# A fused convolution and hard-swish layer: one 256-column matmul ahead of each first layer, and the halves of each pair issued in the other order

## The chip, the cores and the metric

The kernel runs on one core of a Trainium2 chip. The time is what the device takes for one launch, in microseconds (us); the lower the better. The engines are TensorE (PE in the profile; its weight loads are listed apart as PEld), VectorE (DVE), ScalarE (ACT), GpSimd (POOL) and SyncE (SP, which only issues DMAs here). They run side by side and wait for each other through semaphores.

## The reference

```python
# x: 8 x 4096 x 192, weight: 8 heads x 7 taps, w_in: 192 x 2048, w_out: 2048 x 192
w = softmax(weight, axis=-1)
x_pad = zeros(6 rows) ahead of each sequence
attn[b, s, h, g] = sum_k w[h, k] * x_pad[b, s + k, h, g]      # a causal 7-tap convolution
t = attn.reshape(32768, 192)
h = t @ w_in
g = h * clip(h + 3, 0, 6) / 6
out = g @ w_out                                               # 32768 x 192, float32
```

## The kernel before

The 32768 tokens are worked off in 32 blocks of 1024 (NB blocks, TB tokens). A block has three stages: the convolution on VectorE (line 921), the first layer on TensorE (line 508) with its hard-swish on ScalarE and VectorE (lines 302 and 306), and the second layer on TensorE (line 615). Block 0 is special: its weights are still being prepared, and its first layer runs in plain fp32 through `half_mm` (line 296). Blocks 1 to 31 go through `first_layer` and `second_layer` in one loop; the convolution of later blocks runs under the matmuls.

**The two halves of the array.** The 192 input features are laid out as 3 thirds (K3) of 64 partitions. Partitions 0 to 63 hold the first 512 tokens of the block, partitions 64 to 127 the other 512. A matmul of the first layer therefore contracts over 64 rows and uses half of the TensorE array. In the code k is the half: k = 0 is rows 0 to 63, called the upper half of the array in this document, and k = 1 is rows 64 to 127, called the lower half. The two matmuls of a pair (k = 0 and k = 1) go to different halves and to different banks of PSUM, and they can run at the same time.

**The first layer.** `first_layer` walks over 16 chunks n, of 128 hidden features for either half. The first eight use `y_own` (the block's tokens as they lie), the other eight `y_other`, a copy in which the two halves of the partitions are exchanged by DMA. To get fp32 accuracy out of the single-pass data type float32r, activations and weights are split in three parts (HIGH, LOW and MIX), and each chunk needs three products. Each product is one call of `mms`: 3 thirds x 2 halves = 6 matmuls of 64 rows x 512 columns, so three pairs. A chunk has nine pairs and a first layer has 144. Below, pairs are counted from 0 in the order in which they are issued.

`begin(n)` takes a slot of PSUM (two banks), issues HIGH and LOW, and then multiplies both banks by 4097 (line 520, on ScalarE; for the last chunk lines 523 and 524, where VectorE takes one bank). `end(n)` issues MIX onto the multiplied sums and then runs the gate. So MIX of a chunk waits for the multiply, which waits for the last matmul of LOW. The order of the work is written out by hand: begin(0), begin(1), and then end(n) and begin(n + 2) in turn. In pairs: 0 to 5 are HIGH and LOW of chunk 0, 6 to 11 those of chunk 1, 12 to 14 are MIX of chunk 0, 15 to 20 HIGH and LOW of chunk 2, 21 to 23 MIX of chunk 1, and so on. Between begin(0) and end(0) there are the six pairs of begin(1); later there are nine pairs between a chunk's LOW and its MIX.

**The second layer.** It works on column strips of 32 output features (`tile_position=(0, j * 32)`), four streams side by side, in plain fp32.

**Weights.** Each matmul has a weight load of its own, issued ahead of it; the profile shows it as LDWEIGHTS on PEld.

Of the kernel before, what the change touches and what calls it, by code (L numbers as in the profile page):

```python
# [25 lines left out]
def kernel(  # L26
# [8 lines left out]
    nc = tc.nc  # L35
# [7 lines left out]
    N = 512  # L43
    G = 2
    TB = G * N
    D2 = P // 2
# [41 lines left out]
    for base, dma in ((0, nc.scalar), (D2, nc.sync)):  # L88
        dma.dma_start(  # L89
            out=w_sb[base : base + D2],  # L90
# [127 lines left out]
    for n in range(AHEAD):  # L218
# [8 lines left out]
        out=e_sb[:], in0=w_sb[:], in1=mx[:].to_broadcast([P, KC]), op=ALU.subtract  # L227
# [4 lines left out]
    half = cst.tile([P, 1], F32, name="half")  # L232
# [45 lines left out]
    psum = ps.tile([P, 2 * 4, N], F32, name="psum")  # L278
# [22 lines left out]
    def relu(r6, h):  # L301
        nc.scalar.activation(r6, h, ACT.Relu, bias=half[:], scale=1.0 / 6.0)  # L302

    def gate(g_, h):

        nc.vector.scalar_tensor_tensor(  # L306
            out=g_, in0=g_, scalar=1.0, in1=h, op0=ALU.min, op1=ALU.mult
        )
# [93 lines left out]
    def g_sums(engine, which, slots, width):  # L402

        forms = {
            3: (S3, A11, A21, ALU.subtract),
            2: (S2, S1, A11, ALU.subtract), 4: (S3, A12, S2, ALU.subtract),
        }
        for n in which:
            o, a, b, op = forms[n]
            for p in slots[::width]:  # L410
                r = slice(p, p + width)
                engine.tensor_tensor(out=o[:, r], in0=a[:, r], in1=b[:, r], op=op)  # L412
# [42 lines left out]
    def add(out, x, y, op=ALU.add):  # L455
        nc.vector.tensor_tensor(out=out, in0=x, in1=y, op=op)  # L456
# [13 lines left out]
    def r32(ap):  # L470
        return ap.bitcast(F32R)
# [16 lines left out]
    y_own, y_other, pools, s1 = [], [None], [], []  # L488
# [7 lines left out]
    def first_layer(i, jobs):  # L496

        slots = {}

        def both(n):  # L500
            return psum[:, 2 * slots[n] : 2 * slots[n] + 2]

        def mms(n, part, start=False, stop=False):
            group, c = divmod(n, NP)
            for s in range(K3):
                for k in range(2):
                    r = slice(k * D2, (k + 1) * D2)
                    nc.tensor.matmul(  # L508
                        out=psum[:, 2 * slots[n] + k], lhsT=r32(w_in_parts[part][r, c, s]),
                        rhs=r32(y_other[0][r, part, s] if group else y_own[part][r, s]),  # L510
                        start=start and s == 0, stop=stop and s == K3 - 1,
                        skip_group_check=True,
                    )

        def begin(n):
            slots[n] = free_slots.pop(0)
            mms(n, HIGH, start=True)
            mms(n, LOW)
            if n + 1 < count:
                nc.scalar.mul(both(n), both(n), 4097.0)  # L520
            else:
                lower, upper = (psum[:, 2 * slots[n] + k] for k in range(2))
                nc.scalar.mul(lower, lower, 4097.0)
                nc.vector.tensor_scalar(
                    out=upper, in0=upper, scalar1=4097.0, scalar2=None, op0=ALU.mult
                )

        def end(n):
            group, c = divmod(n, NP)
            mms(n, MIX, stop=True)  # L530
            to = g4[:, c, 1:3] if group else g4[:, c, 0::3]
            relu(to, both(n))
            gate(to, both(n))
            free_slots.append(slots[n])

        count = 2 * NP
        begin(0)
        begin(1)
        for job in jobs.get(-1, ()):
            job()  # L540
        for n in range(count):
            if n == count - 3:
                begin(n + 2)
            end(n)
            if n < count - 3:
                begin(n + 2)
            for job in jobs.get(n, ()):
                job()
            if n == 1:
                s1.append(ot.tile([P, NP, N], F32, name="s1", tag="shared")[:])  # L550
            if n < NP and n % 2:
                small_sums(s1[-1], A11, (1, 2, 3, 4), nc.gpsimd, every[n - 1 : n + 1])
            if n > NP and n % 2:
                pair = slice(n - NP - 1, n - NP + 1)
                g_sums(nc.gpsimd if n + 1 < count else nc.vector, (3,), range(NP)[pair], 2)
                if n + 3 < count:
                    nc.gpsimd.dma_start(out=S1[:, pair], in_=A22[:, pair], accum_op=ALU.add)
        for pair in (slice(NP - 2, NP), slice(NP - 4, NP - 2)):
            add(S1[:, pair], A21[:, pair], A22[:, pair])
# [7 lines left out]
    def small_sums(to, x, which, engine=nc.gpsimd, r=every):  # L567

        r = slice(r[0], r[-1] + 1)
        x11, x12, x21, x22 = four_parts(x[:, r])  # L570
        s1, s2, s3, s4 = four_parts(to[:, r])
        forms = {
            1: (s1, x21, x22, ALU.add), 2: (s2, s1, x11, ALU.subtract),
            3: (s3, x11, x21, ALU.subtract), 4: (s4, x12, s2, ALU.subtract),
        }
        for n in which:
            o, p, q, op = forms[n]
            engine.tensor_tensor(out=o, in0=p, in1=q, op=op)  # L578
# [222 lines left out]
    with tc.manual_schedule():  # L801
# [4 lines left out]
            out=c_sb[:], in0=e_sb[:], in1=sm[:].to_broadcast([P, KC]), op=ALU.mult  # L806
# [15 lines left out]
        for _ in range(3):  # L822

            nc.tensor.matmul(
                out=psum[:, b], lhsT=zeros[:, 0:P], rhs=zeros[:], start=True, stop=True
# [57 lines left out]
        slots = [0, 1, 3, 4, 6, 7, 9, 10, 12, 13]  # L883
        n = 3
# [30 lines left out]
        w_in_parts = [late.tile([P, NP, K3, P], F32, name=f"w_in{n}") for n in range(3)]  # L915
# [103 lines left out]
```

## Time and profile before

| | |
|---|---|
| time, median of 3 runs | 2226.65 us (2226.6 to 2228.04) |
| span of the profiled execution, first to last instruction | 2224.9 us |
| mean granted TensorE clock | 0.999 |
| first layer, line 508: matmuls | 8928, 386 and 388 ns each on average |
| second layer, line 615: matmuls of 128x512 on g and w_out | 6712, 552 ns each |
| multiply by 4097, line 520 | 465 on ScalarE, 1008 ns each |
| one block (start of line 508 at 510.08 us to the next at 578.46) | 68.4 us, of which 32.9 in the first layer |

The profile gives matmuls by start and modelled end. The ends of matmuls overlap, since they are pipelined; the pace of the stream is read from start to start. A row of the timeline merges instructions of one kind: start, length from the first start to the last end, engine, line, operation, operands, shape, and how many. In brackets stands the idle time of that engine ahead of the row, and what ended it. In the list of waits each row gives who waited for whom, the total in us, how often, and the longest.

### The profile page before, as it was taken

What the parts mean: (1) busy time and instruction counts of PE and PEld (TensorE: products, weight loads), DVE (VectorE), ACT (ScalarE), POOL (GpSimd) and SP (SyncE); (2) the same over time, 40 slices, a digit from 0 to 9 for tenths busy, and PEclk for the clock granted to TensorE, in tenths of its full rate; (3) what the DMA queues carried; (4) which work ended last, traced back from release to release, by engine and by line L of the source; (5) the groups of instructions that cost most, each with busy time, mean ns of one, the idle gap of its engine ahead of it and who ended that gap; (6) DMA issues with size and microseconds to landing.
All of it is one profiled execution on the core that took longest, in us unless ns stands there. A gap on an engine that the chain in (4) does not pass through costs nothing.

```text
span 2224.9 us, 50339 instructions
## 1 busy us (share of the span) xinstructions
PE 2218.0 (100%) x21496; PEld 1532.7 (69%) x21496; DVE 1894.3 (85%) x1673; ACT 1379.2 (62%) x1678; POOL 823.8 (37%) x690
## 2 busy tenths in 40 slices
PE   9999999999999999999999999999999999999999
PEld 5467776677766777766777667776677776677766
DVE  8888888888888888888888888888888888888876
ACT  7457665576655676555766557665567655576654
POOL 2344432344422444223443234442244422344323
PEclk9999999999999999999999999999999999999999
DMA  6244224443244342344422444324434234442232
GB/s 157 57 98 85 49 58 91 85 83 62 53 82 91 77 80 47 71 91 84 85 48 58 91 87 81 67 49 82 91 79 81 47 67 91 84 84 52 55 77 34
DMA packets 253584, 166.57 MB, mean 75 GB/s; under 512 B 208017, under 2 KB 213137, under 8 KB 253361
## 3 DMA queue, kind: packets, MB, share of 16 engines
q1 hardware_dynamic: 234872, 129.46, 28.4%
q0 software_dynamic: 17248, 33.64, 8.7%
q8 instruction: 168, 2.75, 0.5%
q14 instruction: 56, 0.45, 0.1%
q10 hardware_dynamic: 1240, 0.27, 0.1%
HBM read 31.72 MB, written 25.17 MB: 26 GB/s over the span
## 4 chain that ended last, share of the span: by engine, by line
PE 99%; DVE 0%; DMA 0%; ACTq 0%; issue 0%; DVEq 0%; ACT 0%
PE psum L615 49%; PE psum L508 46%; PE psum L296 2%; PE psum L341 2%; DMA x<-in_x_dram 0%; DVE y L255 0%; DVE top L175 0%; ACTq L89 0%; PE psum L816 0%; DVE results L456 0%; DVE scale L171 0%; DVE y L251 0%; DVE scale L192 0%; DVEq L1014 0%; DVE results L462 0%
## 5 line engine op out<-in xcount | busy, mean ns | idle before, releaser
L615 PE MATMUL psum<-g,w_out 128*32 128x512 f32 (+1 forms) x6712 | 967.5, 552 | 0.0
L306 DVE SCALAR_TENSOR_TENSOR g<-g,psum 128x1024 f32<-128x1024 f32 (+1 forms) x528 | 618.3, 1186 | 198.8 <-ACT g L302 194.5
L578 POOL TENSOR_TENSOR s<-g 128x256 f32<-128x256 f32 x248 | 273.6, 1103 | 1241.1 <-DVE g L306 1200.5
L302 ACT ACTIVATE g<-psum,half 128x1024 f32<-128x1024 f32 (+1 forms) x528 | 564.8, 1087 | 6.0 <-PE psum L508 5.2
L615 PEld LDWEIGHTS psum<-g,w_out 128*32 128x32 f32 x6712 | 371.8, 110 | 246.0 <-issue 126.7
L508 PE MATMUL psum<-y,w_in 64*128 64x512 f32 x4464 | 521.4, 388 | 0.0
L508 PE MATMUL psum<-y_other,w_in 64*128 64x512 f32 x4464 | 516.0, 386 | 0.0
L520 ACT ACTIVATE psum<-psum 128x1024 f32<-128x1024 f32 x465 | 469.0, 1008 | 50.7 <-PE psum L508 48.4
L508 PEld LDWEIGHTS psum<-y,w_in 64*128 64x128 f32 x4464 | 413.5, 184 | 115.7 <-issue 26.0
L508 PEld LDWEIGHTS psum<-y_other,w_in 64*128 64x128 f32 x4464 | 418.1, 184 | 87.8
L615 PE MATMUL psum<-s,w_out 128*32 128x512 f32 (+1 forms) x3272 | 465.5, 570 | 0.0
L921 DVE SCALAR_TENSOR_TENSOR y<-x,c_sb,y 128x1536 f32<-128x1536 f32 x186 | 335.2, 1802 | 2.6 <-ACT y L919 1.3
L412 POOL TENSOR_TENSOR s<-g 128x1024 f32<-128x1024 f32 x93 | 285.9, 3074 | 26.2 <-DVE g L306 26.2
L615 PE MATMUL psum<-g,w_s 128*32 128x256 f32 x1240 | 282.8, 379 | 0.0
L615 PEld LDWEIGHTS psum<-s,w_out 128*32 128x32 f32 x3272 | 154.3, 110 | 81.9 <-issue 49.4
L615 PEld LDWEIGHTS psum<-g,w_s 128*32 128x32 f32 x1240 | 136.4, 110 | 67.7
L412 DVE TENSOR_TENSOR s<-g 128x2048 f32<-128x2048 f32 (+1 forms) x93 | 181.3, 1977 | 1.1
L615 PE MATMUL psum<-s,w_s 128*32 128x256 f32 x744 | 170.7, 379 | 0.0
L578 DVE TENSOR_TENSOR g<-g 128x1024 f32<-128x1024 f32 x124 | 151.7, 1224 | 5.3
L412 DVE TENSOR_TENSOR g<-g 128x2048 f32<-128x2048 f32 x62 | 139.1, 2284 | 0.0
L612 ACT COPY psum<-psum 32x512 f32<-32x512 f32 x93 | 51.3, 551 | 135.4 <-PE psum L615 135.4
L456 DVE TENSOR_TENSOR results<-psum,results 32x256 f32<-32x256 f32 (+3 forms) x128 | 69.3, 541 | 50.9 <-issue 45.5
(91 smaller groups left out, 1299.5 us busy)
## 6 DMA issues: line engine op xcount, KB each, us to landing
y_other<-y SPq DMA_DIRECT2D x186, 384.0 KB, 5.1
g<-g POOLq DMA_DIRECT2D x62, 512.0 KB, 5.0
out_dram<-results SPq DMA_DIRECT2D x378, 64.0 KB, 2.0
x<-in_x_dram SPq DMA_DIRECT2D x53, 388.5 KB, 7.7
stage<-in_moe_w_in_dram SPq DMA_DIRECT2D x16, 192.0 KB, 4.5
stage<-in_moe_w_out_dram SPq DMA_DIRECT2D x8, 384.0 KB, 6.8
x<-in_x_dram SPq DMA_DIRECT2D x7, 384.0 KB, 8.4
x<-in_x_dram POOLq DMA_DIRECT2D x2, 388.5 KB, 5.4
```

Of the source, the lines that this page charges most:

```text
L296: nc.tensor.matmul(out=psum[:, b], lhsT=w[r], rhs=src, start=start, stop=stop, skip_group_check=onto,)
L302: nc.scalar.activation(r6, h, ACT.Relu, bias=half[:], scale=1.0 / 6.0)
L306: nc.vector.scalar_tensor_tensor(out=g_, in0=g_, scalar=1.0, in1=h, op0=ALU.min, op1=ALU.mult)
L341: lambda p=p: nc.tensor.matmul(out=bank[j * QS : (j + 1) * QS, tokens], lhsT=w_out[:, p, w, cols], rhs=x[:, p, tokens], start=(first and p ...
L412: engine.tensor_tensor(out=o[:, r], in0=a[:, r], in1=b[:, r], op=op)
L456: nc.vector.tensor_tensor(out=out, in0=x, in1=y, op=op)
L508: nc.tensor.matmul(out=psum[:, 2 * slots[n] + k], lhsT=r32(w_in_parts[part][r, c, s]), rhs=r32(y_other[0][r, part, s] if group else y_own[ ...
L520: nc.scalar.mul(both(n), both(n), 4097.0)
L578: engine.tensor_tensor(out=o, in0=p, in1=q, op=op)
L612: streams[3].append((t - 0.5, lambda: fn(*args, **kw)))
L615: nc.tensor.matmul(out=out, lhsT=w, rhs=x, start=start, stop=True, tile_position=(0, j * QS), skip_group_check=True,)
L921: jobs.append(lambda k=k: nc.vector.scalar_tensor_tensor(out=y[:], in0=x[:, :, k : k + N], scalar=c_sb[:, k : k + 1], in1=y[:], op0=ALU.mu ...
```

## The change

Ahead of the first pair of each first layer, one more matmul is issued. It goes to the upper half (rows 0 to 63), with the weights and activations of the first real matmul there, but with 256 columns instead of 512. It writes the left half of the bank that the first real matmul of the upper half then overwrites (`start=True`), so its result is not used. And in each pair the lower half (k = 1) is now issued ahead of the upper (k = 0). The changed kernel's lines from here on stand 8 lines further down.

```diff
         def mms(n, part, start=False, stop=False):
             group, c = divmod(n, NP)
+            if n == 0 and start:
+
+                r, half = slice(0, D2), slice(0, N // 2)
+                nc.tensor.matmul(
+                    out=psum[:, 2 * slots[n], half], lhsT=r32(w_in_parts[part][r, c, 0]),
+                    rhs=r32(y_own[part][r, 0, half]), start=True, stop=False,
+                    skip_group_check=True,
+                )
             for s in range(K3):
-                for k in range(2):
+                for k in (1, 0):
                     r = slice(k * D2, (k + 1) * D2)
                     nc.tensor.matmul(
                         out=psum[:, 2 * slots[n] + k], lhsT=r32(w_in_parts[part][r, c, s]),
```

## The prediction

> **What bounds the kernel now.** I read the page's busy times and its chain first, then the groups of line 508, then TensorE's timeline around one first layer, then the list of waits.
>
> ```profile
> PE 2218.0 (100%) x21496; PEld 1532.7 (69%) x21496; DVE 1894.3 (85%) x1673; ACT 1379.2 (62%) x1678; POOL 823.8 (37%) x690
> PEclk9999999999999999999999999999999999999999
> PE 99%; DVE 0%; DMA 0%; ACTq 0%; issue 0%; DVEq 0%; ACT 0%
> L508 PE MATMUL psum<-y,w_in 64*128 64x512 f32 x4464 | 521.4, 388 | 0.0
> L508 PE MATMUL psum<-y_other,w_in 64*128 64x512 f32 x4464 | 516.0, 386 | 0.0
> ```
>
> TensorE is busy over the whole span at an undisturbed clock, and 99% of the chain that ended last is its work, 46% of the span at line 508. So whatever lengthens or shortens TensorE's stream in a first layer is paid at the end. There are 8928 matmuls at line 508, 288 (144 pairs) in each of 31 first layers.
>
> The next answer is TensorE's timeline over the first layer at 510 us, in three cuts: its start with the other engines, its start for weight loads alone, and its second half.
>
> ```profile
> 510.08 2.60 PEld L508 LDWEIGHTS psum<-y,w_in 64*128 64x128 f32 x24 [0.84 <-issue]
> 510.09 3.48 PE L508 MATMUL psum<-y,w_in 64*128 64x512 f32 x28
> ...
> 511.79 1.01 ACT L520 ACTIVATE psum<-psum 128x1024 f32<-128x1024 f32 x1 [1.02 <-PE psum L508]
> ...
> 512.85 1.22 PEld L508 LDWEIGHTS psum<-y,w_in 64*128 64x128 f32 x12 [0.16 <-ACT psum L520]
> ...
> 527.94 15.12 PE L508 MATMUL psum<-y_other,w_in 64*128 64x512 f32 x132
> ```
>
> The last line holds 66 pairs: (15.12 - 0.386) us over 65 steps is 226.7 ns a pair. The first pair's two matmuls are recorded 3 ns apart (510.086 and 510.089 in the single records), and so is every later pair: the halves run in step. In the opening it goes a little slower: pair 5 (counted from 0) starts at 511.348, 1.262 us after pair 0, of which 0.110 is the exposed first weight load, so 230.4 ns a pair.
>
> The middle lines are what matters most here. The multiply of line 520 waits for pair 5, the last of chunk 0's low part (ends 511.743), runs from 511.785 to 512.793, and the weight load of pair 12 (chunk 0's mix part) waits for it until 512.845, with the matmul at 512.948. Without the wait pair 12 would have come at 512.945. That chain is just as long as the six pairs it has to hide behind. It recurs in every block, as the list of waits says:
>
> ```profile
> PEld psum L508 <- ACT psum L520: 5.0, 31, 0.2
> ```
>
> The single records add one thing: the lower half's weight load of pair 12 carries no wait of its own, had a free place since 512.721, and yet is issued at 512.848, 3 ns behind the waiting one. Here nothing passes the load that waits for a semaphore.
>
> **The change, part by part.** (1) The added matmul, 31 times: 256 columns in the upper half (rows 0 to 63). Its weight load takes the place of pair 0's exposed one (110 ns, there before too), and the upper half's real first load hides under it. Its length is not in the trace. Half of a 512-column pair step is 113 ns; at the other end, 256-column matmuls of line 615, which run in plain fp32, follow each other every 216 ns on one column strip. I take 113, the row of the same data type, and keep 216 for the range. The lower half starts pair 0 at the same time as the added matmul, so that from there the upper half trails the lower by about 113 ns.
>
> (2) The offset of the halves. What a pair costs when the halves are half a step apart is not shown for this data type. The nearest rows are the fp32 pairs of line 296 in block 0, same 64-row shape, which ran in step at first and out of step later:
>
> ```profile
> 19.04 1.88 PE L296 MATMUL psum<-y,w_in 64*128 64x512 f32 x8
> ...
> 42.40 0.59 PE L296 MATMUL psum<-y_swapped,w_in 64*128 64x512 f32 x1
> 42.51 0.59 PE L296 MATMUL psum<-y,w_in 64*128 64x512 f32 x1
> 42.83 4.99 PE L296 MATMUL psum<-y_swapped,w_in 64*128 64x512 f32 x22
> ```
>
> In step: (1.88 - 0.596) / 3 = 0.428 us. Apart by 0.11: (4.99 - 0.589 - 0.107) / 10 = 0.429. The offset is neither a gain nor a loss there. Those rows also bound the gain: a step of 429 ns is two passes of 512 columns, 214.6 ns a pass, so at best the 226.7 falls to 214.6. A loss has no row; I bound it by the worst single pair steps of the opening, 236 ns. I take no change.
>
> The Trainium skill's page "TensorE: Matmul & The Clock Gate" (section "Back-to-back issue gap") states N/2.4 + 2.5 ns, 215.8 ns at 512 columns, below this case's 226.7; by it the pair step could fall by 11 ns if being in step is what costs them. The same page (section "What overlaps and what doesn't") says that matmuls start and end strictly in program order, which speaks against the change, since a stall of one half then holds the other.
>
> (3) What becomes of the offset at pair 12. The upper half is now the later one, so pair 5 is finished 113 ns later; line 520 starts 113 ns later, and pair 12's first load, now the lower half's, is released at 512.958 instead of 512.845. The lower half's matmul goes at 513.061, the upper half's load is issued 3 ns behind the released one, and its matmul goes at 513.064. Left to itself the lower half would have started at 512.945 and the upper at 513.058. So the lower half loses the whole 113 ns, the upper half some 6, and **both leave pair 12 in step again**. The remaining 132 pairs of the layer run as before, with the roles of the halves exchanged. If the offset did shorten the first pairs, say to 214.6, pair 5 would come 5 x (230.4 - 214.6) = 79 ns earlier and the delay at pair 12 would be 34 ns, but the halves would be in step just the same: the lower's own time for pair 12 is then earlier still. The offset survives only if a pair takes so long (about 231 ns over the first twelve) that line 520 is no longer late.
>
> (4) The order within pairs. Lower first is the mirror image; I cost it at nothing, on the ground that either half's 144 matmuls at line 508 have the same form. If that ground is gone, rival B prices it.
>
> (5) What hangs on it. Queued behind the waiting load on TensorE is everything; DVE's gates and ACT's next multiplies come later by the same 113 ns. The next such chain has room: pair 21's mix load was issued at 514.795 and its multiply ended at 514.219, 576 ns ahead. The other engines and the DMA queues keep their instructions and their order; nothing is moved past a queue. The first loads that read y_other now wait for the lower half's transfer first, but no wait of line 508 for a DMA stands in the list of waits, so I cost that at nothing; a late transfer would show there.
>
> **Sum.** 113 ns a block x 31 = 3.5 us; from below 34 x 31 = 1.1, from above 216 x 31 = 6.7. TensorE has no idle time in which a block could make it up. The profiled execution's span is 2224.9, 1.75 below the median of the three runs (2226.65), and the same addition holds for both: span 2228.4, time **2230.1 us**, +0.16%. I count as no change what lies within 0.2% (4.45 us, 2222.2 to 2231.1), about what a measurement of this kernel can tell from none.
>
> **The rivals.**
>
> A. The offset lives through the layer and removes what a pair in step has above the best row. Per block 144 x (226.7 - 214.6) = 1742 ns less, 113 more: 1.63 us, x 31 = 50 us, **2176 us**. For it: r32 pairs take 12 ns more per 512 columns than fp32 pairs, and after each exposed load there are some seven irregular pairs (224 to 236 ns) before 226.7 sets in, so small differences in phase do count. Against it: the wait of pair 12 in every block, and the fp32 rows, which gain nothing when apart. It decides if pair 12 leaves more than a few ns between the halves.
>
> B. Slower: with the lower half leading, the irregular state of the opening doesn't settle. Pairs 1 to 7 average 231.5 ns ((511.811 - 510.422) / 6). Over the 132 pairs after the wait that is 132 x 4.8 = 634 ns a block, x 31 = 19.6, with the 3.5 above **2250 us**. For it: the settled 226.7 is a state that the halves fall into after a few pairs, so it hangs on how they start. Against it: they fell into it twice a block in all 31 blocks. It makes the kernel measurably slower from 0.24 ns a pair (0.95 us over 31 x 132 pairs).
>
> C. The added matmul costs more than the half step, 144 ns or more: at 216 it is **2233 us**. A smaller form of the forecast's own mechanism, on the other side of 0.2%.
>
> D. The offset neither dies nor matters: the added matmul's 113 ns once a block, 2230 again; told apart only by the trace.
>
> **How the numbers follow.** Forecast (with D) 0.66, of which 0.07 end above 2231.1 by a dearer start: its own range 2227.5 to 2232. Rival A and smaller gains of its kind 0.13. B and other losses per pair 0.13. C 0.08. Faster 0.13; slower 0.07 + 0.13 + 0.08 = 0.28; same 0.59. The range leaves out A (0.13) and the worst of B (0.06) and so ends at B's 2250; below, it goes to 2225, the forecast's lower bound (2227.7) less the spread of the runs.
>
> **What would show it.** In the timeline of a first layer of the changed kernel (its lines stand 8 further down): 31 matmuls more, with 256 columns; in pairs 0 to 11 the halves some 113 ns apart; the wait of the weight loads for line 520 grown from 0.16 to about 0.27 us in all 31 blocks, in which the upper half's last matmul delays it; after it matmuls in twos 3 ns apart again and 226.7 ns a pair; blocks of 68.49 instead of 68.37 us. The prediction is wrong if the halves are still apart after pair 12, if the step there isn't 226.7, or if the added matmul holds the upper half for much longer than 113 ns.

## The result, and the profile after

The changed kernel takes 2230.22 us in the median against 2226.68 us of the kernel before in the same set of runs: a ratio of 1.0016, with a 95% interval of 1.0009 to 1.0022. That is 3.5 us more, and it lies inside the 0.2% that were taken as no change. The spans of the profiled executions are 2228.3 against 2224.9 us. The times of one and the same kernel scatter by up to 2.0 us between runs and sets of runs (before: 2226.4 to 2228.4), and its spans with them (2224.8 to 2226.6), so where a microsecond matters the period of a block inside the profiled execution is used below: it repeats to the nanosecond in most blocks.

The page of the changed kernel; lines 508, 516 and 528 are now the added matmul, the pairs and the multiply by 4097:

```profile
span 2228.3 us, 50401 instructions
PE 2221.0 (100%) x21527; PEld 1560.8 (70%) x21527; DVE 1894.3 (85%) x1673; ACT 1379.2 (62%) x1678; POOL 823.6 (37%) x690
PEclk9999999999999999999999999999999999999999
PE 99%; DMA 0%; DVE 0%; SPq 0%; ACT 0%; issue 0%; DVEq 0%; ACTq 0%
L516 PE MATMUL psum<-y,w_in 64*128 64x512 f32 x4464 | 524.9, 388 | 0.0
L516 PE MATMUL psum<-y_other,w_in 64*128 64x512 f32 x4464 | 516.1, 386 | 0.0
```

TensorE has 31 matmuls more and is busy 3.0 us longer. The weight loads are busy 28 us longer; 14 of these lie in pairs 0 to 11, where loads of halves that are apart no longer cover each other, and the rest is spread over the whole run and not accounted for. DVE, ACT and POOL are as before. The matmuls on y_other, the second half of each first layer, cost what they did (516.1 us, before 516.0). What changed lies in the first half. The timeline of the same first layer, TensorE and ScalarE:

```profile
510.67 0.18 PEld L508 LDWEIGHTS psum<-y,w_in 64*128 64x128 f32 x1 [0.84 <-issue]
510.67 0.38 PE L508 MATMUL psum<-y,w_in 64*128 64x256 f32 x1
...
512.48 1.01 ACT L528 ACTIVATE psum<-psum 128x1024 f32<-128x1024 f32 x1 [1.13 <-PE psum L516]
...
513.54 0.77 PEld L516 LDWEIGHTS psum<-y,w_in 64*128 64x128 f32 x8
...
528.63 15.12 PE L516 MATMUL psum<-y_other,w_in 64*128 64x512 f32 x132
```

The last row is the same as before to the hundredth: 132 matmuls in 15.12 us, 226.7 ns a pair. The multiply starts 1.813 us after the first matmul of the layer, before 1.699: 114 ns later. The single records show what the rows merge. Each number is the recorded start of a matmul, in ns from the first one of the layer; a matmul that finds its weights not loaded yet is recorded about 110 ns ahead of its work (pair 0, and the lower half's pair 12, whose record lasts 497 ns where 386 is the rule):

```
                pair 0       1       2   ...      10      11        12          13          14         16
before, upper:       0     336     567          2405    2632      2862        3096        3320       3787
before, lower:       3     340     570          2409    2635      2865        3100        3324       3790
after, added:        0
after, lower:        3     338     568          2419    2646      2874+110    3212        3448       3908
after, upper:      223     458     691          2536    2763      2988        3224        3453       3916
```

From pair 0 to pair 11 the halves are 110 to 126 ns apart, with the lower one ahead. Pair 12's weight loads, at 2873 and 2876, come only after the multiply. The lower half's matmul begins work at 2984, the upper one's at 2988: 4 ns apart. From there the halves run together, 3 to 12 ns apart. In 29 of the 31 first layers pair 12 stands at these times to 1 ns; in the other two the halves leave it 2 ns apart, but draw apart over the pairs behind it to 43 ns, and keep these to the last pair. One block takes 68.487 us, before 68.373: 114 ns more, 31 times, 3.5 us.

### The profile page after: what moved, and what is told of

Same layout as the page of the kernel before. It is cut to its first block, busy times and chain, and to the rows that moved or that the text cites. A ratio compares the mean times of both kernels' runs of the same rounds, so it can differ in the third digit from the quotient of the medians.

```text
span 2228.3 us, 50401 instructions
## 1 busy us (share of the span) xinstructions
PE 2221.0 (100%) x21527; PEld 1560.8 (70%) x21527; DVE 1894.3 (85%) x1673; ACT 1379.2 (62%) x1678; POOL 823.6 (37%) x690
## 4 chain that ended last, share of the span: by engine, by line
PE 99%; DMA 0%; DVE 0%; SPq 0%; ACT 0%; issue 0%; DVEq 0%; ACTq 0%
PE psum L623 49%; PE psum L516 46%; PE psum L296 2%; PE psum L341 2%; PE psum L508 0%; DMA x<-in_x_dram 0%; SPq L100 0%; SPq L133 0%; DVE top L175 0%; PE psum L824 0%; DVE y L255 0%; DVE results L456 0%; SPq L89 0%; ACT y L838 0%; ACT scale L186 0%
## 5 line engine op out<-in xcount | busy, mean ns | idle before, releaser
L516 PE MATMUL psum<-y_other,w_in 64*128 64x512 f32 x4464 | 516.1, 386 | 0.0
L516 PEld LDWEIGHTS psum<-y,w_in 64*128 64x128 f32 x4464 | 435.4, 184 | 71.2 <-ACT psum L528 0.3
L516 PEld LDWEIGHTS psum<-y_other,w_in 64*128 64x128 f32 x4464 | 423.8, 184 | 82.1
```

Source lines behind the costliest of these rows:

```text
L516: nc.tensor.matmul(out=psum[:, 2 * slots[n] + k], lhsT=r32(w_in_parts[part][r, c, s]), rhs=r32(y_other[0][r, part, s] if group else y_own[ ...
```

## The experiments

**The order alone.** The kernel before with the lower half first.

```diff
-                for k in range(2):
+                for k in (1, 0):
```

> The lower half first in each pair, without the added matmul. Theory: mirror image, 226.7 ns a pair in step, 2226.7 us. Rival (the order in the pair has a price or gain of its own that is hidden in the 3.5 us): anything over 1 us away from that, with the added matmul then worth the rest.

Span 2224.9 us, as before; a ratio of 0.9999 (0.999 to 1.0009). A block takes 68.373 us, the same to the nanosecond. The halves go into their settled state as they did with the upper half first. So the order in the pair is worth nothing, and rival B has fallen.

**The added matmul alone**, with the upper half first as before.

```diff
-                for k in (1, 0):
+                for k in range(2):
```

> The added matmul with the upper half still first in each pair. The lower half's first matmul then stands in program order behind the upper half's first real one, so the halves never get apart. Theory (the price is the added columns alone): 113 ns a block as in the changed kernel, 2230.2 us, and no longer wait at pair 12 than before (0.16 us). Rival (the price comes from the offset and the longer wait at pair 12): 2226.7 to 2228 us.

Span 2228.3 us, the same 3.4 us above; median 2230.1, a ratio of 1.0009 (1.0 to 1.0019) in a set in which before stood at 2228.05, so 2.0 us by the medians. A block takes 68.480 us, 107 ns more than before, and the wait of the weight loads at pair 12 is in the list nearly as before (5.2 us, 31 times, against 5.0). The price doesn't need the new order. But the expectation was wrong in one thing: the halves did get apart, so this run doesn't show a price without an offset. The records show a second matmul 7 ns after the added one and the next at 224 ns, then one every 115 ns or so; in pair 12 the halves are some 20 ns apart and from pair 13 on 4.

**Which half is which.** The trace doesn't name the half, so the two kernels were run once more with the lower half's matmuls of chunk 0 cut to 508 columns.

```diff
+                    cols = slice(0, N - 4) if n == 0 and k else slice(0, N)
                     nc.tensor.matmul(
-                        out=psum[:, 2 * slots[n] + k], lhsT=...
+                        out=psum[:, 2 * slots[n] + k, cols], lhsT=...
```

> The run with the upper half first and the added matmul, with the lower half's matmuls of chunk 0 cut to 508 columns, so that the trace tells the halves apart; the last 4 columns of the lower half's sums of chunk 0 are left out. In that run the halves got 110 ns apart, which the expectation denied. Reading 1 (the lower half's first matmul starts ahead of the upper half's, which stands before it in program order but finds its half taken): the 64x508 matmul stands 3 to 7 ns after the added one, the upper half's 64x512 some 220 ns after it. Reading 2 (program order holds): the 64x512 first, at 220 ns, and the 64x508 not before it. The time: about 2230 us, as without the marks.

The timeline of the run with the upper half first, cut to the first 0.2 us of a layer:

```profile
510.82 0.38 PE L508 MATMUL psum<-y,w_in 64*128 64x256 f32 x1
510.82 0.49 PE L517 MATMUL psum<-y,w_in 64*128 64x508 f32 x1
```

The 64x508 matmul stands 7 ns after the added one; its record holds the 110 ns of an exposed weight load, so it works from about 117. The upper half's first 64x512 comes at 223 ns, though the program has it ahead of the 64x508. Reading 1 holds: a matmul whose half is free starts ahead of an earlier one whose half is taken, here by 216 ns between the records and by about 106 ns in work. What waits for the results still goes by the program: the upper half's last matmul of pair 5 ends at 1776 ns, the lower half's, which is last in the program and alone carries the signal, at 1630, and the multiply starts at 1821. It didn't run ahead of the slower half. The time was 2231.0 us.

> The changed kernel with the same mark (the lower half's matmuls of chunk 0 with 508 columns; the same 4 columns left out). It shows which half waits at pair 12. Theory: up to pair 11 the upper half's matmuls come some 110 ns after the lower's; at pair 12 the 64x508 matmul is held back by about 113 ns against the 226.7 ns step, the 64x512 by less than 10 ns, and they go 3 to 4 ns apart. Rival (the upper half is held as well): both held back by 100 ns or more and the offset kept. The time: about 2230 us.

At pair 11 the lower half's matmul starts at 2633 and the upper's at 2763. At pair 12 the 64x508 matmul is recorded at 2874 with 110 ns of waiting for its weights, so it works from 2984; it would have been due at 2633 + 227 = 2860 and is held by 124 ns. The 64x512 starts at 2989, 226 ns after its predecessor: not held at all. The two are then 5 ns apart. This is the collapse that the prediction worked out. The time was 2230.16 us.

This run shows one thing more. Over the irregular pairs behind the wait its lower half gets a little ahead once more: 30 ns from pair 16 on. No other weight load of the layer is held up, and in all 31 first layers the halves are still 30 ns apart in the last pair. The second half of the same layer:

```profile
528.54 15.15 PE L517 MATMUL psum<-y_other,w_in 64*128 64x512 f32 x132
```

The row is 0.03 us longer than the 15.12 of the halves in step, which is the offset itself: (15.15 - 0.386 - 0.030) / 65 is 226.7 ns a pair.

**The same columns without an offset.** Two added matmuls, one in each half (against the kernel before; the order in the pairs is that of the changed kernel).

```diff
+            if n == 0 and start:
...
+                for k in (1, 0):
+                    r, half = slice(k * D2, (k + 1) * D2), slice(0, N // 2)
+                    nc.tensor.matmul(
+                        out=psum[:, 2 * slots[n] + k, half], lhsT=...
```

> The changed kernel with an added 256-column matmul ahead of the layer in either half, so that the halves start in step. Theory (the price is the time of the added columns, whether they put the halves apart or not): 31 x 113 ns = 3.5 us above before, as the changed kernel, 2230 to 2231 us where before is 2226.7 to 2228, and the halves 3 ns apart from the first pair on. Rival (the offset and its loss at pair 12 carry part of the price): less than 2 us above before; or, if a second added matmul costs an issue of its own, over 4.5 us above.

Span 2228.4 us, 3.5 above; a ratio of 1.0021 (1.0012 to 1.003). A block takes 68.480 us, 107 ns more. The halves start 3 ns apart and stay so, and the weight loads' wait in pair 12 is that of the kernel before, as the list of waits of this run says:

```profile
PEld psum L509 <- issue: 26.0, 31, 0.8
PEld psum L517 <- ACT psum L529: 5.1, 31, 0.2
```

The added pair takes one step of 113 ns (pair 0 stands 223 ns behind it, of which 110 are the exposed weight load), and the two added matmuls are 3 ns apart, so the second one costs no issue of its own here. So the price is the time of 256 columns, paid at once here and paid through pair 12 in the changed kernel. The times alone would not say so: the medians of this set are 4.5 us apart (2231.24 against 2226.70), just on the rival's line. The profiled execution is the shortest of eleven; the others have spans of 2229.2 to 2229.9 us, and no trace shows where their extra microsecond lies.

**Twice the columns.** The added matmul with 512 instead of 256.

```diff
-                r, half = slice(0, D2), slice(0, N // 2)
+                r, half = slice(0, D2), slice(0, N)
```

> The changed kernel with 512 instead of 256 columns in the added matmul. Theory (the price is the added columns): twice 113 ns a block, 31 x 0.227 = 7.0 us above before, 2233.7 us. Rival (the price is one more instruction and its weight load, whatever its size): 2230.2 us.

Span 2232.2 us, 7.3 above; a ratio of 1.0028 (1.0017 to 1.0039), 6.1 us between the medians of the set. A block takes 68.613 us, 240 ns more against 114 with half the columns. The price goes with the columns, not with the instruction.

**The offset kept alive.** begin(2) is moved ahead of end(0), so that the multiply of chunk 0 has twelve pairs to hide behind. The control is the same move in the kernel before.

```diff
         begin(0)
         begin(1)
+        begin(2)
...
-            if n < count - 3:
+            if 0 < n < count - 3:
                 begin(n + 2)
```

> The changed kernel with begin(2) moved ahead of end(0), so that twelve pairs instead of six lie between the low part of chunk 0 and its mix part, and the wait that put the halves back in step has room. First theory (the offset dies only at that wait, and while it lives a pair takes the 230.8 ns that pairs 1 to 11 of the changed kernel show): halves about 110 ns apart all through the layer, 230.8 ns a pair, so 144 x 4.1 + 113 = 0.70 us a block above before, about 2248 us. Rival 1 (apart, the pairs settle at 226.7 ns as they do in step): 2230 us. Rival 2 (being in step is what costs 12 ns a pair, and the opening pairs were not yet settled): 214.6 ns a pair, about 2176 us. If another wait puts the halves in step, 2229 to 2230 us with the place to be seen in the trace.

> The kernel before with begin(2) moved ahead of end(0): the same reordering without the offset, as the control. Theory: no wait of weight loads for the multiply, and no irregular pairs 12 to 19, which cost some 33 ns a block above 226.7 ns each: 31 x 0.033 = 1.0 us less than before, 2225.7 us. Rival (irregular pairs come from the layer's schedule, not from the wait): 2226.7 us. If the third slot isn't free in time, a new wait at pair 12 and more than 2227 us.

Both are slower than before, for a reason of their own: 2242.77 us, a ratio of 1.0065 (1.005 to 1.008), and 2238.15 us, 1.0045 (1.003 to 1.006). The move takes the wait of pair 12 away and makes a longer one at pair 33, where a slot of PSUM isn't free yet. The list of waits of the run with the offset, and of the control:

```profile
PEld psum L516 <- DVE g L306: 16.0, 31, 0.5
```

```profile
PEld psum L508 <- DVE g L306: 16.2, 31, 0.5
```

So the expected gain of the control was not measured, nor was this offset kept through a whole layer: at pair 33 the matmuls of both halves are held, and leave it 4 ns apart. But up to there it did live, which is what the run was for. The timeline of that stretch, cut to pairs 10 to 29, in one row:

```profile
515.16 4.69 PE L516 MATMUL psum<-y,w_in 64*128 64x512 f32 x39
```

One matmul follows the other every (4.69 - 0.386) / 38 = 113.3 ns, the halves in turn, so a pair takes 226.5 ns apart (226.6 by the single records, which aren't rounded) as it takes 226.7 in step. The opening is slower in this run too (224 to 236 ns a pair up to some 2.4 us into the layer). My first theory, that pairs apart take 230.8 ns, took the opening for the offset; rival 1 of the expectation was right. At the end the offset costs its price as elsewhere: span 2240.0 against 2236.4 in the control, 3.6 us (4.6 by the medians).

**One half alone.** Both matmuls of a pair in the upper half.

```diff
-                    r = slice(k * D2, (k + 1) * D2)
+                    r = slice(0, D2)
```

> The kernel before with both matmuls of each pair in the upper half of the array (rows 0 to 63), one after the other; the lower half does nothing, so the sums of the second 512 tokens are left out and the first ones written twice. It measures the pace of a single half. Theory (a 512-column float32r matmul takes 226.7 ns in its half whether or not the other half runs): 288 x 226.7 = 65.3 us for a first layer, about 3240 us in all. Rival (the 12 ns above the fp32 rows are the price of two halves in step): 214.6 to 216 ns each, 61.8 to 62.2 us for a first layer, 3130 to 3145 us.

It took 3237.75 us, as the theory said. The timeline of the second half of a first layer, cut at 760 us:

```profile
741.29 18.97 PE L508 MATMUL psum<-y_other,w_in 64*128 64x512 f32 x83
```

(18.97 - 0.386) / 82 = 226.6 ns for one matmul with nothing beside it. There is nothing for an offset to win: the 12 ns above half of an fp32 step belong to the stream of float32r matmuls in one half, each with its weight load, and not to two halves in step. The irregular opening is there too with one half alone (224 to 236 ns a step up to 2.4 us, then 226.7).

## Why the prediction was right

**The bound.** Right: TensorE's stream gives back nothing, and 114 ns a block appear as 3.4 us in the span and 3.5 in the median.

**The added matmul (1).** I took 113 ns, half a pair step of float32r. In the changed kernel a block grew by 114. Where the added columns are paid directly (both halves), their step is 113 ns too; the block there grew by 107, because pairs 0 to 11 behind them take 6 ns less than before (2516 against 2522 ns from the start of work). The bound of 216, from the fp32 rows, was far off. (In the table ahead of the prediction the 6712 matmuls of line 615 are two forms: 5440 of 512 columns, 593 ns each, and 1272 of 256 columns, 380 ns.)

**The offset's effect on the pace (2).** Right, and now shown where the prediction had only fp32 rows: 226.5 ns apart, 226.7 in step, 226.6 alone. That an fp32 step is two passes is shown by no run; what is measured is 429 ns, and 214.6 is half of it. With that rival A falls, both its premises: the offset does not outlive pair 12, and there was nothing for it to remove. Of the rule that was cited from the Trainium skill ("TensorE: Matmul & The Clock Gate", section "Back-to-back issue gap"), an estimate of 215.8 ns at 512 columns, no run here shows it for this data type; the measured 226.6 decides.

**The collapse at pair 12 (3).** Right in mechanism and size: the multiply starts 114 ns later, the lower half is held by 111 ns (124 in the marked run, where it is a little further ahead), the upper by none, and they leave 4 to 5 ns apart. Three details were wrong. I expected the wait in the list to grow from 0.16 to about 0.27 us. It fell out of the list instead:

```profile
PEld psum L516 <- ACT psum L528: 0.3, 2, 0.2
```

That is the changed kernel; two of the 31 are left. The list measures the idle time of the weight loads, and leaves out what is not over 150 ns. The load ahead of the wait is now the later half's, at 2539 instead of 2412, and so the idle time between loads shrank from 163 to 150 ns, while the lower half's step from pair 11 to pair 12 grew from 230 to 338 ns.

The second detail is how slow the pairs would have to be for the offset to survive: I wrote about 231 ns, but from the start of the upper half's pair 5 to that of the lower half's pair 12 the chain takes 1.60 us, and with the offset of 0.113 it has seven pairs to hide behind, so 245 ns a pair would be needed (246 with the measured 1261 and 2984). The slowest single step in the opening of the kernel before is 236, so the collapse was safer than I thought.

The third detail is the premise that matmuls start in program order, cited from the same page of the Trainium skill, "TensorE: Matmul & The Clock Gate" (section "What overlaps and what doesn't"). The measurement contradicts it for starts: across the halves a later matmul was recorded 216 ns ahead of an earlier one and worked about 106 ns ahead of it. My expectation for the added matmul alone, that the halves would stay together, failed by it. The collapse doesn't rest on it. It rests on the weight load that waits for the semaphore, and that did hold the load behind it: 2873 and 2876.

**The order (4).** Right: 0.0 us. (The threshold given with rival B, 0.24 ns a pair, is 0.23 by its own sum; nothing hangs on it.)

**Rivals C and D.** The added matmul cost 114 ns, under C's 144. D can't be told from the forecast by the time, as said; the trace shows that the offset died at pair 12. That an offset which doesn't die would not matter either is shown by the 30 ns of the marked run.

**What stays open.** After the start of a layer and after the wait of pair 12 a few pairs take 224 to 236 ns (up to 244 in the runs with added columns) before 226.7 sets in. At the start this is so in step, apart and with one half alone, so the halves are not its cause. They follow the waits: with begin(2) moved ahead, in the control, pairs 12 to 19 take 226 to 227 ns and the irregular ones (224 to 236) come after the wait at pair 33 instead. What makes them was not tried.

## What to carry to other kernels

Before putting two streams out of step, measure one of them alone: where it runs no faster by itself, there is nothing to win by moving it. An offset lives only until the first wait without room on which both streams hang (pair 12 here, pair 33 with begin(2) moved, none for the 30 ns of the marked run), so follow the waits of the layer first, and look for the one that has no room. On an engine that is never idle, useless work costs about its own time, however it gets lost in between: 107 to 114 ns a block here for a step of 113.

## What the runs showed of the hardware

- A 64-row float32r matmul of 512 columns takes 226.6 ns alone in its half of the array, and 226.5 to 226.7 with the other half busy, in step, 30 ns apart or half a step apart. The fp32 matmuls of the same shape took 429 ns, in step or 107 ns apart.
- Matmuls of different halves can start out of program order: one was recorded 216 ns, and worked about 106 ns, ahead of an earlier one whose half was busy. The signal of the last matmul of pair 5 still came only after the slower half: it ended at 1630 ns, the earlier one at 1776, and the multiply started at 1821.
- A weight load that waits for a semaphore holds a load for the other half behind it, though that half had room: in the kernel before, room since 512.721 us and issued at 512.848, 3 ns behind the waiting load.
